# Running-sum rows read in six pieces, and two row copies of an attention and spectral-mix kernel cut into transfers of six, six and four partitions

## The chip, the core and the metric

The kernel runs on one core of one Trainium2 chip. The metric is the device time of one execution in microseconds (us), taken as the median of several runs. The core has the engines PE (TensorE), ACT (ScalarE), DVE (VectorE), POOL (GpSimd) and SP (SyncE), and 16 DMA engines that carry every transfer. A transfer is issued by SP or by POOL; the profile keeps the two apart as DMA queues: q1 "hardware_dynamic" holds what SP issues, q0 "software_dynamic" what POOL issues, and q8 and q14 "instruction" hold the chip's own fetching of instructions.

## What is computed

Inputs are `q`, `k`, `v` of shape (8 batches, 8 heads, 576 tokens, 64), `s` of shape (8, 8, 576), and the weights `w_r`, `w_i` (64 modes, 512, 512) and `w_ch` (512, 512), all float32. The reference, cut to what matters:

```python
cum = np.cumsum(np.maximum(s, 0), axis=-1)
bias = -(cum[:, :, :, None] - cum[:, :, None, :])
scores = where(causal, -1e9, q @ k.T / 8 + np.minimum(bias, 0))
x = softmax(scores) @ v                      # heads side by side: (8, 576, 512)
X = np.fft.rfft(x, axis=1)[:, :64]           # 64 modes of the tokens
Y = X * (w_r + 1j * w_i)                     # a complex 512x512 product per mode
u = x + np.fft.irfft(Y, n=576, axis=1)
out = u + np.maximum(u @ w_ch, 0)            # float32 (8, 576, 512)
```

The two mode weights are 134 MB of float32 and are read once.

## The kernel before, in words

**Attention, 32 steps (L591 to L625).** Step `n` works on one batch and two heads. `qt` and `kt` (two buffers each) hold the transposed q and k in partitions 0 to 63. Partition 64 of `qt` holds the negative running sum of `s` as an extra row, and partition 64 of `kt` holds ones, so that one product gives score and bias together (L397). ACT takes the exponential (L405), PE multiplies by v (L433), DVE divides (L438 to L448), and `fft` (L450) multiplies by sines and cosines and leaves the modes in `xs`.

**The running-sum row.** The sums are made once in `ncum_sb` (64 pairs of batch and head, 576 numbers of bf16). For steps 0 and 1 SP copies the rows from there (L345). L586 writes all of `ncum_sb` to `ncum_dram` in DRAM, and for each of the steps 2 to 31 `cum_rows` (L336) lets SP copy the step's two rows of 1152 bytes from DRAM into partition 64 of `qt` (L342). That copy waits until PE has read the old row out of the buffer; it is issued one step ahead.

**The weights.** The weights come in half chunks of 8 modes by 128 input channels (512 KB each as bf16), cast on the way. POOL issues them at L243 in the order of use into rings of 5 and 3 buffers, a load waiting until PE has read the buffer's old content. A list worked out ahead (L247 to L269) sets how many may be issued before each attention step. Each such load lies on all 16 DMA engines, 16 packets of 2048 bytes on each and a 4-byte packet that reports the end. `modes(g, c)` (L470) multiplies chunk `c` (8 chunks) of channel group `g` (4 groups).

**The end (L626 to L965).** Of the last channel group, chunks 0 to 5 are done in the loop at L862, chunk 6 at L883 and chunk 7 at L897. A chunk's product `yb` (128 rows: 16 mode rows by 8 batches, 512 columns) is transposed (L698), multiplied by `w_ch` (`y_times_wch`, L706) and stored as `vb`. For the inverse transform the rows have to lie as 16 partitions by 8 batches in `yv[partition, batch, which, column]`, where `which` is 0 for y and 1 for y times `w_ch`. `spread(c, which, rows)` (L511) makes that change of layout with one SP transfer, 128 pieces of 1024 bytes from 128 partitions to 16. It is called for `which` = 1 of chunks 4, 5, 6, 7 (L714, L915) and for `which` = 0 of chunks 6 and 7 (L506). Chunks 0 to 3, and `which` = 0 of chunks 4 and 5, go by PE instead (`gather`, L717).

**Order around the change.** SP issues in program order: the row copies, five small constants, then the spreads, then the stores of the result (L854, L857). PE's order in the end is written out: in the products of chunk 7 (`modes` with `meanwhile`), after the first half of the four groups of products (those with `w_r`), it runs `first_z` for the first two pairs of output tiles, which reads `yv` rows 0 to 95 with `which` = 1 (L773), that is chunks 0 to 5, then the third group of products, then `first_u`, then the fourth. All products of chunk 7 read weights that are loaded last: the two `w_r` halves, then `w_i` in four pieces of 256 KB.

Of the kernel before, what the change touches and what calls it, by code (L numbers as in the profile page):

```python
# [11 lines left out]
BF16 = mybir.dt.bfloat16  # L12
# [6 lines left out]
def kernel(  # L19
# [11 lines left out]
    nc = tc.nc  # L31
    B, H, S, D = q.shape
# [6 lines left out]
    NPAIR = B * H  # L39
# [6 lines left out]
    MC = 8  # L46
    NCK = NM // MC
# [12 lines left out]
    HP = P // 2  # L60
# [53 lines left out]
    auxpool = aux.enter_context(tc.tile_pool(name="aux_psum", bufs=2, space=PSUM, side="right"))  # L114

    dpool = ctx.enter_context(tc.tile_pool(name="dram", bufs=1, space=bass.MemoryType.DRAM))
    ncum_dram = dpool.tile([NPAIR, S + HP], BF16, name="ncum_dram")
    at = ExitStack()
    ap_ = at.enter_context(tc.tile_pool(name="attn", bufs=1))
    qkpool = at.enter_context(tc.tile_pool(name="qk_sb", bufs=2))  # L120
# [2 lines left out]
    ncum_sb = ap_.tile([NPAIR, S], BF16, name="ncum_sb")  # L123
    NQ = 2
    qt = [ap_.tile([P, 2, S], BF16, name=f"qt{i}") for i in range(NQ)]
# [25 lines left out]
    def loads_qk(n):  # L151

        if n >= N:
            return []
        g, b = divmod(n, B)
        hs = slice(2 * g, 2 * g + 2)
        t = loaded[n] = loaded[n + 1] = qkpool.tile([P, 2, R * D], BF16, name="qk2", tag="qk2")
        return [
            (
                t[HP * i : HP * i + HP, x0:x1],  # L160
                src[b + x0 : b + x1, hs].rearrange("b h (p r) d -> (h p) b (r d)", r=R),
            )
            for x0, x1 in ([(0, 2)] if n else [(0, 1), (1, 2)])
            for i, src in enumerate((q, k))
        ]

    def loads_v(n):

        if n >= N:
            return []  # L170
        g, b = divmod(n, B)
        return [
            (
                v2[n % NV][:, : 2 * NWN * W].rearrange("p (w h c) -> p w h c", w=NWN, h=2)[:, :, h, P:],
                v[b, 2 * g + h, : NF * P, :].rearrange("(w p r) d -> p w (r d)", p=P, r=2),
            )
            for h in range(2)
        ]

    def loads_tails(g):  # L180

        if g >= NG:
            return []
        return [
            (
                v4[g % 2][NL * h : NL * h + NL, :, :D],
                v[:, 2 * g + h, NF * P :, :].rearrange("b t d -> t b d"),
            )
            for h in range(2)
        ]  # L190
# [22 lines left out]
    def loads_w(upto):  # L213
        todo = []
        while 2 * len(wt) < min(upto, 2 * len(wq)):
            k = len(wt)
            g, c, ri = key = wq[k]
            i = ring_of(k)
            if i is None:
                halves_, t = early[k], whole[k] if k < len(whole) else None  # L220
            else:
                t = (wpool, wpool2)[i].tile([P, UM, DM], BF16, name="w_sb", tag="w")
                halves_ = [t[:, x * WM : x * WM + WM] for x in range(2)]
            if k == len(wq) - 1:
                t = None
            src = (moe_w_r, moe_w_i)[ri]
            for m0, m1, d in [(0, MC, t)] if t is not None else [(0, WM, halves_[0]), (WM, MC, halves_[1])]:
                for h in range(2):
                    first = 1 if ri == 1 and c == 0 and m0 + h == 0 else 0
                    todo.append((  # L230
                        d[HP * h : HP * h + HP, 2 * first :].rearrange("p (m q) e -> p m (q e)", q=2),
                        src[
                            c * MC + m0 + h + 2 * first : c * MC + m1 : 2, g * P : (g + 1) * P, :
                        ].rearrange("m (p q) e -> p m (q e)", q=2),
                    ))
            wt[key] = halves_
        return todo

    def load(*lists):

        todo = [((i + 0.5) / len(l), x) for l in lists for i, x in enumerate(l)]
        for _, (dst, src) in sorted(todo, key=lambda t: t[0]):
            nc.gpsimd.dma_start(out=dst, in_=src)  # L243
# [41 lines left out]
    with tc.tile_pool(name="cum_psum", bufs=1, space=PSUM) as cpsum:  # L285
# [3 lines left out]
        for t in qt + kt:  # L289
# [3 lines left out]
            out=cum, data0=spos, data1=zer, initial=0.0, op0=ALU.add, op1=ALU.add  # L293
# [16 lines left out]
        for x in range(2):  # L310
            rows = slice(NL * x, NL * x + NL)
            nc.vector.tensor_copy(
                out=cumt4[rows, :], in_=cumt_sb[rows, NK, x::2]
# [14 lines left out]
    def pad_p():  # L328
        for i in range(NP_):
            for x in range(NK):  # L330
                nc.vector.memset(
                    p_sb[i][:, poff[x] + S - x // 2 * W : poff[x + 1]], 1.0 if x in (0, NK - 1) else 0.0
                )


    def cum_rows(n):  # L336
        if n >= N:
            return
        g, b = divmod(n, B)
        p0 = b * H + 2 * g  # L340
        if n >= 2:
            nc.sync.dma_start(out=qt[n % NQ][D : D + 1, :, :], in_=ncum_dram[p0 : p0 + 2, :S].unsqueeze(0))  # L342
            return
        for h in range(2):
            nc.sync.dma_start(out=qt[n % NQ][D : D + 1, h, :], in_=ncum_sb[p0 + h : p0 + h + 1, :])  # L345

    def transposes(n, half):
        if n >= N:
            return
        src = loaded[n][:, n % 2, :].rearrange("p (r d) -> p r d", d=D)[:, half * RH : half * RH + RH]  # L350
        ps = trpool.tile([P, RH, 2 * RP], BF16, name="tr_ps", tag="tr")
        for r in range(RH):
            for i in range(2):
                rows = slice(HP * i, HP * i + HP)
                nc.tensor.transpose(ps[rows, r, :], src[rows, r, :], ident16[rows, rows])  # L355
        for i, dst in enumerate((qt, kt)):
            copy = (nc.vector.tensor_copy, nc.scalar.copy)[half * i]
            to = dst[n % NQ][:D].rearrange("d h (p r) -> d h p r", r=R)
            copy(  # L359
                out=to[:, :, :, half * RH : half * RH + RH],  # L360
                in_=ps[HP * i : HP * i + HP].rearrange("d r (h p) -> d h p r", h=2),
            )
# [147 lines left out]

    def spread(c, which, rows):  # L511

        nc.sync.dma_start(out=yv[16 * c : 16 * c + 16, :, which, :], in_=rows)

# [60 lines left out]
    def mode_products(n, half=None):  # L577
        cs = mode_steps.get(n, [])
        for c in cs if half is None else cs[2 * half : 2 * half + 2]:
            modes(c // NCK, c % NCK)  # L580

    with tc.tile_pool(name="sc_psum", bufs=2, space=PSUM) as scpool, \
            tc.tile_pool(name="tr_psum", bufs=1, space=PSUM) as trpool, \
            tc.tile_pool(name="av_psum", bufs=1, space=PSUM) as avpool:
        cum_rows(0)
        nc.sync.dma_start(out=ncum_dram[:, :S], in_=ncum_sb)  # L586
        transposes(0, 0)
        transposes(0, 1)
        load(loads_qk(2) + loads_v(2))
        pad_p()  # L590
        for n in range(N):  # L591
            if n in (0, 2):
                nc.vector.memset(xs_flat[n // 2].bitcast(FP32), 0.0)
            tails_due = loads_tails(n // B + 1)[n % B - 3 : n % B - 2] if 2 < n % B < 5 else []
            load((loads_qk(n + LA) if n % 2 else []) + loads_v(n + LA) + tails_due, loads_w(on_chip[n]))
            if n == N // 2 + 1:
                nc.gpsimd.dma_start(out=wch_sb, in_=moe_w_ch.rearrange("(dt p) e -> p dt e", p=P))
            cum_rows(n + 1)
            scores(n, 0)
            av(n - 1, 1)  # L600
            if n and n % B == 0:
                scores(n, 1)
                fft(n - 1)
                av(n, 0)
                mode_products(n, 0)
                transposes(n + 1, 0)
                mode_products(n, 1)
                transposes(n + 1, 1)
                continue
            mode_products(n)  # L610
            transposes(n + 1, 0)
            scores(n, 1)
            i = first_pairs[n - N + len(first_pairs)] if n >= N - len(first_pairs) else None
            if i is not None:
                first_transposed(i, 0)
            transposes(n + 1, 1)
            fft(n - 1)
            av(n, 0)
            if i is not None:
                first_product(i, 0)  # L620
                first_transposed(i, 1)
            if i is not None:
                first_product(i, 1)
        av(N - 1, 1)
        fft(N - 1)  # L625
# [5 lines left out]
    yv = finpool.tile([P, B, 2, DM], FP16, name="yv")  # L631
# [250 lines left out]
    c = NCK - 2  # L882
# [25 lines left out]
    for cols in halves:  # L908
        vp = auxpool.tile([P, DM // 2], FP32, name="v_ps", tag="aux")
        for dt in range(DT):  # L910
            nc.tensor.matmul(
                vp, yt[:, dt, :], wch_sb[:, dt, cols], start=(dt == 0), stop=(dt == DT - 1)
            )
        nc.vector.tensor_copy(out=vb[:, cols], in_=vp)
    spread(NCK - 1, 1, vb)  # L915
    for cols in halves:
        for i in range(NPRE):
# [78 lines left out]
```

## Time and profile before

| What | Value |
|---|---|
| median of 3 runs (lowest to highest) | 441.62 us (440.95 to 442.10) |
| the profiled execution: its own time / its span | 442.11 us / 440.3 us |
| PE, DVE, ACT, POOL busy | 77%, 57%, 51%, 39% of the span |
| DMA: bytes written, mean rate | 93.30 MB, 212 GB/s |
| HBM read, written | 163.58 MB, 9.51 MB |
| packets of POOL's queue q0 / of SP's queue q1 | 61424 / 7592 |
| packets of instruction queues q8 / q14 | 34 / 13 |
| granted TensorE clock, mean | 0.925 |

The span runs from the first to the last instruction; the 1.81 us beyond it lie around the execution. The page's second part cuts the span into 40 slices of 11 us, its fourth part follows the work that ended last back from the end, and its sixth lists DMA issues with their time to landing. Times in the text are us from the start of the span. Beside these views the trace keeps a record of each DMA packet (start, duration, size, queue, but not the DMA engine it ran on), of each landing (the increment of a transfer's semaphore that a DMA engine makes when its share is in place) and of the granted clock.

### The profile page before, as it was taken

What the parts mean: (1) busy time and instruction counts of PE and PEld (TensorE: products, weight loads), DVE (VectorE), ACT (ScalarE), POOL (GpSimd) and SP (SyncE); (2) the same over time, 40 slices, a digit from 0 to 9 for tenths busy, and PEclk for the clock granted to TensorE, in tenths of its full rate; (3) what the DMA queues carried; (4) which work ended last, traced back from release to release, by engine and by line L of the source; (5) the groups of instructions that cost most, each with busy time, mean ns of one, the idle gap of its engine ahead of it and who ended that gap; (6) DMA issues with size and microseconds to landing.
All of it is one profiled execution on the core that took longest, in us unless ns stands there. A gap on an engine that the chain in (4) does not pass through costs nothing.

```text
span 440.3 us, 10592 instructions
## 1 busy us (share of the span) xinstructions
PE 340.8 (77%) x4409; PEld 203.7 (46%) x4409; DVE 252.5 (57%) x574; ACT 226.0 (51%) x421; POOL 171.7 (39%) x257
## 2 busy tenths in 40 slices
PE   1588999899695977973939458899987797778995
PEld 1365666465463644641616125556554345432341
DVE  7667776677573555752715315766655344450795
ACT  1387878267463634860727024766651334330794
POOL 6555454424353444323444343433322212310293
PEclk9999999999988888995968767999999989996999
DMA  9999999999999999999999999999999999996498
GB/s 179 207 206 206 204 206 208 207 209 207 207 205 207 210 207 210 207 209 208 205 209 208 209 208 209 207 210 206 210 211 212 212 211 211 203 218 121 155 381 347
DMA packets 69063, 93.30 MB, mean 212 GB/s; under 512 B 25932, under 2 KB 27592, under 8 KB 69016
## 3 DMA queue, kind: packets, MB, share of 16 engines
q0 software_dynamic: 61424, 81.28, 104.6%
q1 hardware_dynamic: 7592, 11.36, 7.2%
q8 instruction: 34, 0.56, 0.5%
q14 instruction: 13, 0.11, 0.1%
HBM read 163.58 MB, written 9.51 MB: 393 GB/s over the span
## 4 chain that ended last, share of the span: by engine, by line
DMA 53%; PE 25%; DVE 15%; issue 3%; POOL 2%; ACT 1%; DVEq 0%; POOLq 0%
DMA w_sb<-in_moe_w_i_dram 21%; DMA w_sb<-in_moe_w_r_dram 17%; DMA qk<-in_k_dram 8%; DMA qk<-in_q_dram 5%; PE sc_ps L397 3%; DVE xs L468 3%; DVE qt L359 3%; PE z_ps L681 3%; PE yp L478 3%; DVE x_all L443 2%; PE av_ps L433 2%; PE sc_ps L391 2%; PE tr_ps L355 2%; DVE xt L553 2%; PE z_ps L773 2%
## 5 line engine op out<-in xcount | busy, mean ns | idle before, releaser
L405 ACT ACTIVATE p_sb<-sc_ps,cumt_sb 128x576 f16<-128x576 f32 (+1 forms) x256 | 141.9, 636 | 21.8 <-PE sc_ps L397 21.4
L397 PE MATMUL sc_ps<-qt,kt 128*128 128x512 bf16 (+2 forms) x384 | 76.8, 312 | 6.9 <-ACT kt L359 6.1
L243 POOL DMA_DIRECT2D v<-in_v_dram x72 | 51.4, 714 | 60.6 <-DMA w_sb<-in_moe_w_i_dram 12.8
L243 POOL DMA_DIRECT2D w_sb<-in_moe_w_i_dram x62 | 38.5, 623 | 89.2 <-DMA w_sb<-in_moe_w_i_dram 28.3
L359 DVE COPY qt<-tr_ps 64x576 bf16<-64x576 bf16 x64 | 47.8, 747 | 41.5 <-PE tr_ps L355 41.5
L478 PE MATMUL yp<-w_sb,xs 128*32 128x512 bf16 (+1 forms) x480 | 42.2, 431 | 29.1 <-DMA w_sb<-in_moe_w_i_dram 25.4
L355 PE MATMUL tr_ps<-ident,qk 64*64 64x64 bf16 x1152 | 34.3, 205 | 33.8 <-DMA qk<-in_k_dram 16.0
L243 POOL DMA_DIRECT2D w_sb<-in_moe_w_r_dram x60 | 37.4, 624 | 53.0 <-DMA w_sb<-in_moe_w_r_dram 33.3
L397 PEld LDWEIGHTS <-kt 128*128 128x128 bf16 x384 | 38.3, 105 | 34.5 <-ACT kt L359 12.8
L391 PE MATMUL sc_ps<-negm,ident 128*128 128x256 bf16 x256 | 53.5, 293 | 0.1
L355 PEld LDWEIGHTS <-qk 64*64 64x64 bf16 x1152 | 26.4, 117 | 51.7 <-DVE kt L359 20.3
L376 ACT ACTIVATE p<-sc_ps,cumt 128x64 f16<-128x64 f32 x32 | 10.1, 314 | 73.8 <-PE sc_ps L372 73.6
L433 PE MATMUL av_ps<-v,p_sb 128*128 128x65 f16 x1024 | 44.2, 197 | 1.8 <-DVE x_all L443 0.6
L359 ACT COPY kt<-tr_ps 64x576 bf16<-64x576 bf16 x32 | 22.8, 714 | 40.8 <-DVE qt L359 40.1
L433 PEld LDWEIGHTS <-p_sb 128*128 128x128 f16 x1024 | 37.4, 100 | 9.6 <-DVE x_all L443 5.4
L468 DVE CAST xs<-ft_ps 64x128 bf16<-64x128 f32 x128 | 36.7, 287 | 7.3 <-PE ft_ps L458 5.7
L478 PEld LDWEIGHTS <-xs 128*32 128x32 bf16 (+1 forms) x512 | 17.8, 146 | 46.0 <-DMA w_sb<-in_moe_w_i_dram 24.6
L438 DVE TENSOR_REDUCE den<-av_ps 128x5 f32<-128x10 f32 x64 | 10.8, 169 | 48.3 <-PE av_ps L433 47.3
L443 DVE TENSOR_TENSOR x_all<-av_ps,rcp 128x320 f16<-128x320 f32 x64 | 31.5, 492 | 2.2
L498 DVE TENSOR_TENSOR y_acc<-yp,y_acc 128x512 f32<-128x512 f32 x16 | 11.1, 692 | 29.2 <-PE yp L478 28.5
L539 ACT COPY z<-z_ps 128x512 f32<-128x512 f32 x22 | 12.9, 586 | 26.9 <-PE z_ps L571 14.2
L458 PE MATMUL ft_ps<-Ff_sb,x_all 128*64 128x192 f16 (+1 forms) x320 | 24.4, 266 | 1.0 <-DVE x_all L443 1.0
(107 smaller groups left out, 439.4 us busy)
## 6 DMA issues: line engine op xcount, KB each, us to landing
w_sb<-in_moe_w_r_dram POOLq DMA_DIRECT2D x60, 512.0 KB, 13.6
w_sb<-in_moe_w_i_dram POOLq DMA_DIRECT2D x55, 512.0 KB, 13.2
out_dram<-r_w SPq DMA_DIRECT2D x16, 512.0 KB
v<-in_v_dram POOLq DMA_DIRECT2D x72, 64.0 KB, 11.1
qk<-in_q_dram POOLq DMA_DIRECT2D x15, 288.0 KB, 12.0
qk<-in_k_dram POOLq DMA_DIRECT2D x15, 288.0 KB, 13.2
x_all<-in_moe_w_r_dram POOLq DMA_DIRECT2D x4, 512.0 KB, 8.4
w_sb<-in_moe_w_i_dram POOLq DMA_DIRECT2D x3, 384.0 KB, 12.7
```

The costliest lines, as they stand in the source:

```text
L243: nc.gpsimd.dma_start(out=dst, in_=src)
L355: nc.tensor.transpose(ps[rows, r, :], src[rows, r, :], ident16[rows, rows])
L359: copy(out=to[:, :, :, half * RH : half * RH + RH], in_=ps[HP * i : HP * i + HP].rearrange("d r (h p) -> d h p r", h=2),)
L391: nc.tensor.matmul(ps[:, bass.ds(w * S, W)], ident16, negm[:, bass.ts(r, W)], start=True, stop=False, skip_group_check=True,)
L397: nc.tensor.matmul(ps[:, c0 : c0 + i1 - i0], keys[:, w, r, :], qh[:, i0:i1], start=False, stop=True, skip_group_check=True,)
L405: nc.scalar.activation(out=pt[:, poff[x] : poff[x] + S - w * W], in_=ps[:, w * S : (w + 1) * S - w * W], func=ACTF.Exp, bias=cumt_sb[:, x, ...
L433: nc.tensor.matmul(ps[:, I, r : r + NCH], lhsT, rhs, start=(i == 0), stop=(i == len(todo) - 1), skip_group_check=True,)
L443: nc.vector.tensor_tensor(out=x_all[:, g, b, :, D * h : D * h + D], in0=ps[:, :, 1 : NCH], in1=rcp.unsqueeze(2).to_broadcast([P, NT, D]), ...
L458: nc.tensor.matmul(ps[HP * q_ : HP * q_ + HP].rearrange("p h f -> p (h f)"), x_all[:nT, g, b, T, q_::2], Ff_sb[:nT, T, :], start=(T == 0), ...
L468: nc.vector.tensor_copy(out=xs[g % 2][HP * h : HP * h + HP, q_, :, h, :, b, :], in_=a)
L478: nc.tensor.matmul(ps[32 * cg : 32 * cg + 32, :], cols[k0:, q_, 1 - ri, :, c * MC // 2 + cg], wt[(g, c, ri)][cg // 2][k0:, 2 * (cg % 2) + ...
L681: nc.tensor.matmul(zs[i, x], xts[i][:, x, dt, :], wch_sb[:, dt, :], start=(dt == 0), stop=(last and dt == DT - 1), skip_group_check=True,)
```

## The change

The copy `ncum_dram` in DRAM is laid out anew: each pair's 576 sums stand in three pieces of 192, 224 numbers apart. Writing it takes 192 pieces of 384 bytes instead of 64 of 1152. The copy into `qt` takes a step's two rows as six pieces of 384 bytes, where it took two of 1152. `spread` is cut for chunks below 6, which are chunks 4 and 5 of `which` = 1: three transfers with 6, 6 and 4 of the 16 target partitions (48, 48 and 32 source rows), where there was one with 16. SP issues 57 instructions instead of 54. Nothing is changed in what the other engines execute; the instructions that wait for a spread wait for three semaphores instead of one.

```diff
-    ncum_dram = dpool.tile([NPAIR, S + HP], BF16, name="ncum_dram")
+    NE6 = 6
+    CP = 2 * S // NE6
+    ncum_dram = dpool.tile([NPAIR, S // CP, CP + 32], BF16, name="ncum_dram")
...
-            nc.sync.dma_start(out=qt[n % NQ][D : D + 1, :, :], in_=ncum_dram[p0 : p0 + 2, :S].unsqueeze(0))
+            nc.sync.dma_start(
+                out=qt[n % NQ][D : D + 1, :, :],
+                in_=ncum_dram[p0 : p0 + 2, :, :CP].rearrange("h x t -> (h x) t"),
+            )
...
     def spread(c, which, rows):
 
-        nc.sync.dma_start(out=yv[16 * c : 16 * c + 16, :, which, :], in_=rows)
+        cuts = (0, 2 * MC) if c >= NCK - 2 else (0, NE6, 2 * NE6, 2 * MC)
+        for r0, r1 in zip(cuts, cuts[1:]):
+            nc.sync.dma_start(
+                out=yv[2 * MC * c + r0 : 2 * MC * c + r1, :, which, :], in_=rows[B * r0 : B * r1, :]
+            )
...
-        nc.sync.dma_start(out=ncum_dram[:, :S], in_=ncum_sb)
+        nc.sync.dma_start(
+            out=ncum_dram[:, :, :CP], in_=ncum_sb.rearrange("c (x t) -> c x t", t=CP)
+        )
```

## The prediction, made before the result was known

> **What bounds the kernel now.** I read the page's slices first. The DMA row is full from the first microseconds to about 402 us, while no compute engine is (PE is highest, 77%):
>
> ```profile
> PEclk9999999999988888995968767999999989996999
> DMA  9999999999999999999999999999999999996498
> ...
> q0 software_dynamic: 61424, 81.28, 104.6%
> q1 hardware_dynamic: 7592, 11.36, 7.2%
> q8 instruction: 34, 0.56, 0.5%
> ```
>
> So the weight stream of POOL sets the pace, with SP's queue and the instruction fetches beside it on the same DMA engines. Next I asked who waits for the last weights, in the chain of waits from 379 us on:
>
> ```profile
> 382.36 0.77 POOL w_sb L243 x2
> 383.13 0.44 issue
> 383.57 15.64 DMA w_sb<-in_moe_w_r_dram
> 399.21 0.14 issue
> 399.35 1.09 PE yp L478 x6
> 400.44 0.96 PE z_ps L773 x2
> ...
> 404.11 1.00 PE yp L478 x4
> ...
> 406.55 0.60 PE yp L478 x4
> ```
>
> The columns are start, length, what. The second `w_r` half of chunk 7 lands at 399.21; from 399.35 PE works without a gap to 407.15, and the rest of the kernel hangs on that. The weights used after it (last landing 405.13, needed at 406.55) have 1.4 us to spare. PE had been idle for 1.87 us before 399.35 (its last product, v_ps L709, ends at 397.48), so an earlier landing is worth its full amount up to 1.87 us.
>
> Then the landings. A weight load lands 16 times, once per DMA engine. For loads issued at 34.36, 367.91 and 383.57, sorted (us; the bars are mine):
>
> ```
> 34.36 41.43 41.52 41.59 41.61 41.62 41.80 | 41.89 41.92 | 41.93 41.97 41.98 42.15 42.27 42.82 42.84 43.17
> 367.91 382.86 382.91 382.94 383.44 383.76 384.09 | 385.31 385.42 | 386.58 386.78 387.09 387.22 387.39 387.41 387.46 387.48
> 383.57 394.84 395.00 395.00 395.06 395.12 395.49 | 396.25 396.68 | 397.35 397.73 398.00 398.18 398.21 398.22 398.24 399.21
> ```
>
> A load is placed only when its **slowest** engine is done. Over the kernel the engines have drifted into six early ones, a pair, and eight late ones. The packet records say why. A row copy of L342 lands on two engines; its 1152-byte packet holds the next weight packet off by 60 ns, its report packet by 22: 30 copies x 82 ns = 2.5 us on one fixed pair. From the first row to the second the pair fell behind the six by 1.7 us (from 0.31 to 2.03, means), with 27 copies between: 2.2 by that price. The 34 instruction fetches (16 KB, nearly 1 us each) repeat their durations with a period of eight (974, 961, 893, 892, 949, 945, 935, 974 ns), so they seem to go round eight engines: the late ones.
>
> **The change part by part.**
>
> *The spreads of chunks 4 and 5.* These two run inside the wait for the last weights:
>
> ```profile
> 384.21 6.46 SPq L513 DMA_DIRECT2D yv<-v_sb  x2
> ...
> q0 software_dynamic: 248, 0.48, 93.1%
> q1 hardware_dynamic: 144, 0.13, 18.1%
> ```
>
> (the first line is from the timeline, the others from the DMA queues at 388 to 390.7 us: SP's 128 pieces and 16 reports pass among the weight packets). Now each lands 16 times, so each DMA engine carries 8 pieces. Weight packets start 154 ns apart on one engine; with pieces between they start 208 apart: 54 ns a piece. Per engine and spread 8 x 54 + 22 for the report = 0.45 us, for both 0.91. A check: the eight late engines land on average at 387.18 and 398.14 in the lower rows, 10.96 us for four loads, where undisturbed loads land 2.48 apart (9.92): 1.04 too long, the 0.91 and something of a fetch at 390.25.
>
> A copy of two rows lands on 2 engines and a transfer to 16 partitions on 16, so I take it that 6, 6 and 4 partitions land on 6, 6 and 4, always from the same end of the engines, where the row pair is too. Then ten engines carry no piece (**-0.91 us**), two carry 16 per spread instead of 8 (16 pieces and 2 reports more in all, +0.9 us), and four carry 24 (32 pieces and 4 reports more, 32 x 54 + 4 x 22 = +1.8 us). If those six are the pair and four of the early six, the late eight gain 0.91 and the others have room, worked out next.
>
> *The rows in six pieces.* The pair is relieved of 60 + 22 ns per copy and six engines get a 384-byte piece. Packets of that size took 22 to 35 ns at the start of the kernel: with the report 44 to 57 ns, x 30 = 1.3 to 1.7 us on six engines. The pair gains about 1.0, the four lose 1.5. Room: at 367.91's row the early six stand 3.4 to 4.6 us ahead of the last. They ran dry at 382.9 to 384.1, as the next load was issued at 381.76 and first landed at 386.71 (2.5 of work, so begun at 384.2), which swallows about 1 of the 1.5. In the last row they come to about 395.0 + 0.5 + 1.8 = 397.3, the pair to 396.5 - 1.0 + 1.8 = 397.3, the late ones to 399.21 - 0.91 = 398.3. Still last: the late ones. So this edit buys nothing by itself; it makes room for the other. The rows themselves land 4.5 us after issue, one step (6.6 us or more) ahead, and in the waits of PE no L397 waits for them: their cover is some 5 us. Writing `ncum_dram` is 12 x 22 instead of 4 x 64 ns per engine: nothing, 15 us before the first read (7.7 and 22.9).
>
> *SP.* Four issues more at 0.55 to 0.6 us. SP's next work after 391.9 is the y spread of chunk 6 at 395.34: 3 us of cover. Without it that spread would be late, which PE reads only after 411.
>
> *The new wait.* `first_z` waits for three transfers of chunk 5 instead of one; behind it on PE stands all that follows. Now chunk 5's pieces start at 393.94 (3.27 us after the issue ends) and land by 396.42. After: 24 pieces in one line at 208 ns end at 398.93, reports and landing (0.5) make 399.4 to 399.5. PE will want them at 398.45 + 1.09 = 399.54. That fits by 0.1 us. From below: faster pieces when weights run dry, no loss; from above, see the second rival. I take 0 to 0.1 lost.
>
> **Sum:** 442.11 (execution; span 440.3 and 1.81 around it) - 0.91 + 0.05 = 441.25. The profiled run lies 0.49 above the median, so for the median 441.62 - 0.86, rounded **440.7**.
>
> **A rule against it.** The Trainium skill, "DMA: Bandwidth & Descriptors", Rules for kernel authors, says to put a multiple of 16 outermost, since a smaller outermost dimension confines the DMA to that many engines. By it alone the cut triples a spread's time on its engines (1.67 to 5.0 us by this trace's 208 ns) for nothing. The same page (why a DMA increments its semaphore by 16) says that such a transfer takes the lowest-numbered engines; the trace agrees as far as the same pair is always hit, but it gives no numbers.
>
> **Rivals.**
>
> *Slower: the pieces hit late engines.* Nothing here shows that the other four of the six belong to the early group; only that pair and fetch engines are distinct, and that neighbours would be natural. If one of the four is late, it comes at 398.24 + 1.5 + 1.8 = 401.5 instead of 399.21: PE starts 2.3 us later, up to 3.3 if it is the straggler. Time 443.9 to 444.9. It decides as soon as one such engine has less than 3.3 us of lead. Chance 0.12.
>
> *The pieces come too late for `first_z`.* If two weight packets pass per piece (54 + 308 = 362 ns), 24 pieces end at 402.6: PE then waits past 400.44 for some 2.7 us, 444.2. Against it: 1:1 was seen on all engines. Chance 0.05; each 0.1 us beyond 399.54 costs 0.1.
>
> *More than forecast: the clock.* In these stages (span, PE, PEld, DVE, ACT, POOL busy, then granted clock):
>
> ```profile
> 387.50:399.20 11.70, 7.28 (x86) 3.34 (x84) 6.04 (x9) 2.89 (x5) 0.60 (x1) 0.96 1.12 218
> 399.20:407.20 8.00, 7.78 (x34) 2.12 (x34) 0.03 (x1) 0.00 (x0) 0.00 (x0) 0.63 0.44 92
> ```
>
> PE, having idled, got half the clock from 398.33 to 405.15. If the shorter pause (0.97 for 1.87 us) avoids that, PE's part shrinks until the last weights bind (405.13 - 0.9 = 404.2 against 405.65): up to 1.4 us more, 439.3. Chance 0.16. This state may also differ from run to run (440.95 to 442.10).
>
> *Nothing.* The straggler, 1 us behind the other late engines, carries a fetch; if fetches move with the change, the 0.91 may drown: 441.6. Chance 0.07.
>
> **How the numbers follow.** Forecast 0.60, range 440.0 to 441.4. This kernel's measurement can tell about 0.3% (1.3 us) from no change, so the likeliest gain of 0.9 us lies inside it. Faster by more, so below 440.3: 0.20 of the forecast's 0.60 and 0.15 of the clock case, together 0.35. Slower: 0.12 + 0.05 = 0.17. Within: the remaining 0.40 of the forecast, 0.07 and 0.01, together 0.48. The range takes in clock case and half of the late-piece case: 439.3 to 443.0.
>
> **What would show it.** Right: the load now landing last at 399.21 lands at about 398.3; its 16 landings are closer together, with no pair apart; PE's idle time before yp L478 drops to 1.0 us; SP's pieces land on 6, 6 and 4 engines. Wrong: PE waits at z_ps L773 for yv; the first landings of a load lie as before while the last move out; or the slices of the tail change.

## The result, and the profile after

| | before | after |
|---|---|---|
| median (lowest to highest, executions) | 441.88 us (440.32 to 442.75, 13) | 443.82 us (442.57 to 445.22, 13) |
| ratio to before | | 1.0046, 95% interval 1.0034 to 1.0058 |
| first profiled execution: time / span | 442.11 / 440.3 us | 442.57 / 440.8 us |

The change costs 0.46%, 1.9 us; the interval leaves out 1, so this is a loss, if a small one. The first trace of the changed kernel is of its quickest execution, so what it shows is less than the whole.

From the page of the changed kernel, the clock, the DMA row and the queues:

```profile
PEclk9999999999987988895977758999997999996998
DMA  9999999999999999999999999999999999995498
...
q0 software_dynamic: 61424, 81.28, 104.4%
q1 hardware_dynamic: 7960, 11.36, 7.3%
q8 instruction: 34, 0.56, 0.5%
```

SP's queue has 368 packets more (7592 before), the shares have moved by 0.2 points at most, and the DMA row is as full as before. SP issues 76 transfers in the trace instead of 72, four more and not three. Averages over the span cannot show what happened; the chain of waits does (start, length, what):

```profile
382.29 17.80 DMA w_sb<-in_moe_w_r_dram
400.10 0.14 issue
400.23 1.09 PE yp L483 x7
401.32 0.97 PE z_ps L784 x2
...
406.76 0.60 PE yp L483 x4
```

The same load still ends the wait, but it lands at 400.10, not 399.21, and the forecast was 398.3. The timeline of PE has PE's idle time before it (in brackets), first before the change and then after it; the forecast was 1.0:

```profile
399.35 1.09 PE L478 MATMUL yp<-w_sb,xs 128*32 128x512 bf16 x8 [1.87 <-DMA w_sb<-in_moe_w_r_dram]
400.23 1.09 PE L483 MATMUL yp<-w_sb,xs 128*32 128x512 bf16 x8 [2.88 <-DMA w_sb<-in_moe_w_r_dram]
```

The stages of the prediction, cut at the new landing (span, PE, PEld, DVE, ACT, POOL busy, clock, DMA share, GB/s):

```profile
387.50:400.10 12.60, 6.42 (x68) 2.73 (x68) 5.83 (x9) 2.89 (x5) 0.59 (x1) 0.90 1.11 213
400.10:407.40 7.30, 7.10 (x34) 2.11 (x34) 0.02 (x1) 0.00 (x0) 0.00 (x0) 0.70 0.35 73
```

The first stage is 0.9 us longer, at nearly the same rate (213 and 218 GB/s). The second is 0.7 shorter with the same 34 matmuls, at a clock of 0.70 instead of 0.63: in this execution most of the delay is paid back by the clock, which is taken up below.

Now the landings of that load, one per DMA engine, sorted (us; the bars are mine). The first row was shown in the prediction:

```
before   394.84 395.00 395.00 395.06 395.12 395.49 | 396.25 396.68 | 397.35 397.73 398.00 398.18 398.21 398.22 398.24 | 399.21
after    393.18 393.23 393.69 395.12 395.44 396.57 | 397.57 397.73 397.87 397.90 397.95 398.12 398.12 398.79 | 399.88 400.10
```

The late pack ends about where it ended before (the prediction wanted it 0.91 earlier), and **two engines now stand two microseconds behind it**; one of them decides. Before, one engine alone stood that far back, 1.7 us.

### The profile page after: what moved, and what is told of

Same layout as the page of the kernel before. It is cut to its first block, busy times and chain, and to the rows that moved or that the text cites. A ratio compares the mean times of both kernels' runs of the same rounds, so it can differ in the third digit from the quotient of the medians.

```text
span 440.8 us, 10555 instructions
## 1 busy us (share of the span) xinstructions
PE 338.7 (77%) x4362; PEld 203.9 (46%) x4409; DVE 252.7 (57%) x574; ACT 226.3 (51%) x421; POOL 171.3 (39%) x257
## 4 chain that ended last, share of the span: by engine, by line
DMA 50%; PE 25%; DVE 16%; issue 4%; ACT 2%; POOL 2%; DVEq 0%; POOLq 0%
DMA w_sb<-in_moe_w_i_dram 25%; DMA w_sb<-in_moe_w_r_dram 16%; DMA qk<-in_k_dram 5%; PE yp L483 4%; DVE xs L473 3%; DVE qt L364 3%; PE sc_ps L402 3%; DMA qk<-in_q_dram 3%; DVE x_all L448 2%; PE z_ps L692 2%; PE av_ps L438 2%; PE sc_ps L396 2%; PE tr_ps L360 2%; DVE xt L562 2%; PE z_ps L784 2%
## 5 line engine op out<-in xcount | busy, mean ns | idle before, releaser
L402 PE MATMUL sc_ps<-qt,kt 128*128 128x320 bf16 (+2 forms) x337 | 66.4, 302 | 10.3 <-ACT kt L364 5.8
```

The lines of the kernel that those rows point to most:

```text
L402: nc.tensor.matmul(ps[:, c0 : c0 + i1 - i0], keys[:, w, r, :], qh[:, i0:i1], start=False, stop=True, skip_group_check=True,)
```

## The experiments

The prediction's rival "the pieces hit late engines" had nearly come true in size (443.9 to 444.9 for it, 443.82 measured). Three theories went into the runs. **A**: among the six engines that carry the small pieces are some of the late ones, so the load lands later. **B**: the pieces of chunk 5 land too late and PE waits for them at `z_ps`, or the small transfers cost as such. **C**: the clock; PE idles longer and works longer at half speed. A began as "one late engine, the last of all" and became "three" after the first four runs; the expectations below carry the version of their time. The packet records support one, as is shown below.

Each run is compared with runs of the kernel before on the same chip; "load" is the second `w_r` half of chunk 7.

**The rows alone.** The change with `spread` as before.

```diff
-        cuts = (0, 2 * MC) if c >= NCK - 2 else (0, NE6, 2 * NE6, 2 * MC)
+        cuts = (0, 2 * MC)
```

> Only the rows in six pieces; the spreads are whole as before. Theory A (one of the six engines that carry small pieces is a late one, the last of all): that engine gets 30 x 35 to 57 ns = 1.0 to 1.7 us more row work and draws the stream of loads back; the load issued near 368 lands last about 0.4 to 0.6 us later than before's 387.48, as it did in the changed kernel (388.05), the second w_r half of chunk 7 at 399.6 to 399.9 (before 399.21), time +0.3 to +0.7 us. Theory B (the small transfers of the spreads cost as such, whatever engines they land on): nothing, within 0.2 us of before. Theory C (the clock): landings as before, and a time that differs only by how long the granted clock stays at half.

Measured: 441.50 us against 441.40, ratio 1.0002 (0.9990 to 1.0014). In time the rows cost nothing and bring nothing, as the prediction had it; A's +0.3 to +0.7 for them failed, B's zero held. The trace is a lesson by itself: its load landed at 400.09, as late as in the changed kernel and even later than A said (399.6 to 399.9), yet the time was 441.30. PE, at half clock, was busy with v_ps until 400.47, and the clock came back at 402.08. One trace does not tell whether the rows by themselves make the load late in most executions.

**The spreads alone.** Before, with chunks 4 and 5 cut 6, 6, 4.

```diff
-        nc.sync.dma_start(out=yv[16 * c : 16 * c + 16, :, which, :], in_=rows)
+        cuts = (0, 2 * MC) if c >= NCK - 2 else (0, 6, 12, 2 * MC)
+        for r0, r1 in zip(cuts, cuts[1:]):
+            nc.sync.dma_start(
+                out=yv[2 * MC * c + r0 : 2 * MC * c + r1, :, which, :], in_=rows[B * r0 : B * r1, :]
+            )
```

> Only the spreads of chunks 4 and 5 in 6, 6 and 4; rows as before in two pieces on the pair. Theory A: the late engine among the six carries 16 pieces per spread instead of 8, 16 x 54 + 2 x 22 ns = +0.9 us, the late ones outside the six lose 0.9; the last landing of the second w_r half lies at 399.1 (carrier in the middle of the late group) to 400.1 (carrier is the last), time -0.1 to +0.9 us; together with rows_only it adds up to the changed kernel's +1.9 within 0.7. Theory B: the whole +1.9 us is here, with chunk 5's pieces landing at 399.6 to 400.2 and PE waiting for them at z_ps, or the load landing at 400.1 as in the changed kernel. If all six had room, as the prediction took it: load at 398.3, time -0.8.

Measured: 443.71 against 441.40, ratio 1.0051 (1.0035 to 1.0066). A loss as large as the whole is here. In the trace the load lands at 400.30 and chunk 5's last piece at 400.39. It is not two engines that stand apart here: five land between 399.67 and 400.30.

**Four engines instead of six.** Rows in four pieces, both spreads in four transfers of 4 partitions (one execution).

```diff
-    NE6 = 6
+    NE6 = 4
...
-        cuts = (0, 2 * MC) if c >= NCK - 2 else (0, NE6, 2 * NE6, 2 * MC)
+        cuts = (0, 2 * MC) if c >= NCK - 2 else (0, 4, 8, 12, 2 * MC)
```

> Four engines in place of six everywhere: rows in four pieces of 576 bytes, both spreads in four transfers of 4 partitions, so 64 pieces of the spreads on each of four engines. Theory A with a late engine as fifth or sixth: the late engines carry no piece, the second w_r half lands at 398.2 to 398.6 (before 399.21, changed kernel 400.10); but chunk 5's pieces, 32 in a line, land near 401.7 to 402.5 (24 took 6.4 to 7.0 us from 393.2 on), so PE waits for yv at z_ps, time +1.3 to +2.2 us. If a late engine is already among the first four: the load at 400.1 or later. Theory B: no earlier landing of the load than in the changed kernel.

Measured: 445.98. From its chain of waits:

```profile
398.52 4.76 DMA yv<-v_sb
403.28 0.34 issue
403.62 1.01 PE z_ps L784 x2
```

Now PE waits for `yv`, as expected. More telling are the 16 landings of the load:

```
four     394.60 394.66 394.75 395.42 | 397.12 397.17 397.28 397.30 397.34 397.40 397.48 397.65 | 398.04 398.28 398.72 399.51
```

Eight engines land within 0.5 us around 397.34, their mean. That is 9.30 us after the load four places ahead was complete (388.04); in the three traces of before the late pack, without its straggler, comes 10.51, 9.95 and 10.46 us after it. The pack has gained 1.0 us on average. Counted from the mean of the late eight of that earlier load instead, it is 10.08 against 10.80, 10.55 and 10.80, a gain of 0.6. Either way it goes towards the 0.91 that the prediction gives to engines without pieces: **these eight carry none**, so no late engine is among the first four. Of the engines that come first, four land as if untouched (394.60 to 395.42).

**Which engines they are.** Before, with seven extra copies to an unused place in DRAM, of 1 to 7 partitions of 1280 bytes.

```diff
+    probe = dpool.tile([N, 8, NT * P + 64], FP16, name="probe")
...
+            if n > N - B:
+                kp = n - (N - B)
+                nc.sync.dma_start(
+                    out=probe[n, :kp, : NT * P], in_=x_all[:kp, NG - 1, (n - 1) % B, :, :].rearrange("p t d -> p (t d)")
+                )
```

> The kernel before with seven extra copies to an unused place in DRAM, at attention steps 25 to 31, of 1, 2, ... 7 partitions of 1280 bytes. They land on 1 to 7 engines, so the k-th engine of the order is held up by 8-k copies of about 60 + 22 ns. Theory A: the landings of the load issued near 368 and the reports of the loads behind it show the first three or four tagged engines in the early group and the pair, the fifth or sixth tag in the late group. The prediction's assumption: six tags on the pair and early engines, and only the seventh late. The time is that of before within 0.5 us.

Measured: 441.28 in one execution, inside the 440.04 to 442.73 of before: no cost that shows. An engine that works without a break sends its report packets 2.486 us apart, load after load, so the 16 can be followed one by one. The copy of six partitions passes at 318.0 to 318.3 us, and exactly six engines fall behind, by 0.05 to 0.07 us. Two report intervals each, engines in the order in which the load issued at 305.67 landed on them (us; "fetch" marks an engine that an instruction fetch at 321.64 holds up as well):

```
place  1    2    3    4    5    6    7    8    9    10   11   12     13   14   15   16
       4.97 5.04 5.04 4.97 4.97 5.03 5.04 5.04 4.97 4.97 4.97 fetch  5.04 4.97 4.97 4.97
```

Places 2, 3, 6, 7, 8 and 13. Five of the six belong to the eight that land first, among them both engines of the row pair: the row copy at 310.43 holds up places 6 and 8. **One, place 13, belongs to the late half.** An expectation below has places 1, 6, 7, 8, 9 and 13 (counted there from 0) and three late ones; that took 1 for 2, whose reports lie 25 ns apart, and 9 for 3, 6 ns apart. But place 3 lands 5.05 us apart from the load issued at 305.67 to the one at 308.61 (314.86 and 319.91), place 9 4.97 (317.36 and 322.33). The landings of the change and of `four` say the same as the packets: with `four`, four early engines come as if untouched, in all five traces of the change three (in the first 393.18 to 393.69, the next at 395.12). So of the fifth and sixth engine one is early and one is late.

**Chunk 4 alone, twice.** The cut only for `c == NCK - 4`, rows as before.

> Only the spread of chunk 4 in 6, 6 and 4; chunk 5 whole, rows as before. Theory A (three of the six engines that a six-partition transfer lands on belong to the late half, as the extra copies showed: places 0, 5, 6, 7, 8 and 12 of 16 by landing): the late ones among the six carry 16 or 24 pieces of chunk 4 instead of 8, +0.45 to +0.9 us, the other late ones lose 0.45; the second w_r half lands 0.4 to 0.9 later, time +0.4 to +1.0 us, that is a part of the +2.2 of both. Theory B (the pieces of chunk 5 come too late for PE): nothing, since chunk 5 is whole; time within 0.3 us of before or up to 0.4 below.

> Chunk 4 alone in 6, 6 and 4, a second comparison: if the gain is real, -0.2 to -0.9 us (ratio 0.998 to 0.9995); if it was chance, within 0.2 us of before.

Measured: 441.31 against 441.81, ratio 0.9986 (0.9975 to 0.9997), and then 441.64 against 441.55, ratio 1.0001 (0.9989 to 1.0014). The gain did not come back on the second chip: an interval that just misses 1 is no find. The load landed at 399.06 and 398.98. A's +0.4 to +1.0 failed: by the prediction's price chunk 4's pieces bring 8 more to the late engine, 0.45 us, which need not reach past the engine that stands behind the others anyway (1.6 to 1.8 us in the three traces of before).

**Chunk 4 in four transfers of 4.**

> Chunk 4's spread in four transfers of 4 partitions, chunk 5 whole, rows as before: 32 pieces on each of four engines, none on twelve. Theory A: of the four engines one or two belong to the late half; they get 24 x 54 + 3 x 22 ns = +1.4 us instead of +0.9 at most, so the second w_r half lands at 399.3 to 400.0 and the time is 0 to +0.8 us of before, above c4_only. If only the twelve relieved engines count (they lose 0.45 us): -0.4 to -0.8 us as in c4_only.

Measured: 441.46 against 441.55, ratio 1.0000 (0.9987 to 1.0014). It tells nothing apart.

**Chunk 5 alone.** The cut only for `c == NCK - 3`.

> Only the spread of chunk 5 in 6, 6 and 4; chunk 4 whole, rows as before. Theory A: as for chunk 4, +0.4 to +1.0 us, and the two together make the +2.2. Theory B: nearly all of the +2.2 is here; the third transfer lands at 399.5 to 400.5 and PE waits for it at z_ps, or the pieces of the three transfers run into the last weights and stretch their packets.

Measured: 442.41 against 441.81, ratio 1.0024 (1.0008 to 1.0040). In its trace (443.89 us) the load lands at 400.77, and the chain shows the second rival of the prediction at work:

```profile
392.44 9.75 DMA yv<-v_sb
402.18 0.05 issue
402.23 1.03 PE z_ps L777 x2
```

PE had come there at 402.00 (400.77 + 0.14 + 1.09), so that wait cost 0.2 us, not the whole. For the late load A has no price: 8 pieces more are 0.45 us here as with chunk 4 alone, where the load landed 1.7 us earlier.

**The price of late pieces by themselves.** Before, with chunk 5's whole spread issued behind chunk 6's y spread.

```diff
+    spread(NCK - 3, 1, vb5)
```

(ahead of the second chunk's transposes, at L883, and left out of `y_times_wch` for chunk 5)

> The kernel before, with the whole spread of chunk 5 issued after chunk 6's y spread, some 6 us later: it lands on all 16 engines at about 401 to 402.5. No piece of it lies ahead of the second w_r half, which lands at 398.5 to 398.9. Theory B: PE waits at z_ps for yv until 401 to 402.5, and the time is +0.7 to +2 us: the price of late pieces alone. Theory A: no loss, 0 to -0.5 us.

Measured: 445.52 against 441.78, ratio 1.0086 (1.0065 to 1.0107). In PE's timeline, the load's wait is short and the one for `yv` long (idle time in brackets):

```profile
398.81 1.09 PE L478 MATMUL yp<-w_sb,xs 128*32 128x512 bf16 x8 [0.69 <-DMA w_sb<-in_moe_w_r_dram]
402.96 1.01 PE L774 MATMUL z_ps<-yv,G_sb 96*128 96x512 f16 x2 [3.07 <-DMA yv<-v_sb]
```

With no piece of chunk 5 ahead of it, the load lands at 398.67, 0.5 us before its mean of 399.22 in before: what B costs when it is really there, and what 8 pieces per engine are worth.

**Taking B away.** PE's order changed in both kernels: `first_u` before the third group of products, `first_z` behind it, so that chunk 5 is read some 4 us later.

```diff
-    yb = modes(NG - 1, NCK - 1, {2: lambda: (first_z(0), first_z(1)), 3: first_u})
+    yb = modes(NG - 1, NCK - 1, {2: first_u, 3: lambda: (first_z(0), first_z(1))})
```

> The kernel before, with PE's first_z moved behind the third group of products of chunk 7 and first_u in its place: the rows of chunk 5 are then read about 2 us later (at about 402.5 to 403). Baseline for the next run. Since the third group may wait for its w_i quarters (landed 401.5 and 402.3), time between 0 and +1.5 us of before.

> The changed kernel with the same reordering of PE. The pieces land as in the changed kernel (chunk 5's third transfer at 400 to 402.2), but PE wants them only at about 402.5. Theory B (PE waits for chunk 5's pieces in most executions, though not in the two that were traced): the distance to the reordered kernel before shrinks from +1.9 to 0 to +0.6 us. Theory A (the loads land later, since late engines carry the pieces): the distance stays at +1 to +2, as the w_i loads are late by the same.

Measured against the same runs of before: 441.30, ratio 0.9995 (0.9977 to 1.0012), and 443.22, ratio 1.0040 (1.0025 to 1.0054). The distance stays at 1.9 us though `first_z` no longer waits; from the chain of the reordered changed kernel:

```profile
382.27 18.43 DMA w_sb<-in_moe_w_r_dram
400.69 0.14 issue
400.83 1.08 PE yp L483 x6
...
405.19 0.54 PE z_ps L784 x2
```

Chunk 5's last piece had landed at 400.52, 4.7 us before PE reads it. **The wait of B is not the cause.** The load lands at 400.69, against 399.50 in the reordered kernel before. B's other half, that the small transfers cost as such, is not ruled out by this; it comes back with the long packets at the end.

**Rows and chunk 4.** The change with chunk 5 whole.

> The change without its cut of chunk 5: rows in six pieces, chunk 4 in 6, 6 and 4, chunk 5 whole. c4_only took 0.14% (0.6 us) off and the rows nothing; so 440.9 to 441.6, that is -0.2 to -0.8 us against before, and 2 to 2.5 below the change. If the loss of the change lay in the sum of all pieces on six engines, +0.5 or more.

Measured: 442.58 against 441.78, ratio 1.0022 (1.0009 to 1.0036). Slower by 0.8 us where the parts gave nothing; in its trace (441.76, one of its quickest) the load lands at 399.38, as in before. I have no cause for it.

**More traces of the two kernels.**

> The kernel before, once more, for a second trace: how far do the landing of the second w_r half (399.21) and the half clock of TensorE (398.33 to 405.15) move from one execution to the next? If the clock alone sets the spread of 440.0 to 442.7, the landings agree within 0.3 us and the time follows the length of half clock between 399 and 407.

> The kernel before, third trace: the second w_r half at 399.0 to 399.5, chunk 5's pieces by 396.5, time 440.5 to 442.5.

> The changed kernel, once more, for a second trace, since its first was of its quickest execution (442.57 against a median of 443.82). Theory A: the second w_r half lands at 400 to 401.5, and PE stands still before it by the difference. Theory C: the landing agrees with the first trace (400.10) and the difference in time is that of the half clock behind it.

> The changed kernel, third trace. In an execution near the median (443.8), theory A: the second w_r half lands at 400.7 to 401.8, and PE goes on with it 0.14 us later; theory B: it lands near 400.1, and PE stands at z_ps until a landing of yv at 401.5 to 402.5; theory C: landings near 400.1 and 400.2, and the clock at half for 2 us or more longer between 400 and 408.

> The changed kernel, fourth trace, with the same three outcomes as the third.

> The changed kernel, fifth trace, with the same three outcomes as the third.

With the first of each, in us:

| trace | time | load lands | last two engines behind the pack | half clock | y of chunk 7 done |
|---|---|---|---|---|---|
| before | 442.11 | 399.21 | 0.8, 1.7 | 398.33 to 405.15 | 407.13 |
| before, second | 441.47 | 399.08 | 0.7, 1.6 | 396.93 to 403.75 | 406.48 |
| before, third | 442.57 | 399.36 | 0.7, 1.8 | 395.69 to 405.93 | 407.58 |
| after | 442.57 | 400.10 | 2.0, 2.2 | 397.59 to 404.42 | 407.33 |
| after, second | 442.18 | 400.04 | 1.9, 2.1 | 400.92 to 404.33 | 406.96 |
| after, third | 443.46 | 400.46 | 1.3, 2.6 | 398.74 to 405.56 | 408.23 |
| after, fourth | 444.15 | 401.06 | 2.0, 3.1 | 396.25 to 406.49 | 408.77 |
| after, fifth | 443.61 | 400.21 | 1.8, 2.0 | 396.40 to 406.64 | 408.37 |

The pack is the seven engines ahead of the one before the last two, their mean. In before one engine stands 1.6 us or more behind it, in four of the five traces of the change two do, in the third one. Whether they are the same engines from trace to trace the landings do not tell, nor which of them carries pieces; in the reordered kernel before, without any cut, two stand apart as well (1.5 and 2.1). B shows in one of the five, the third, by 0.28 us ("issue" is the wait for chunk 5's last piece, landed at 401.75):

```profile
400.60 1.08 PE yp L483 x6
401.68 0.28 issue
401.95 1.01 PE z_ps L784 x2
```

In the other four the pieces were there (399.98 to 400.27) before PE asked (400.84 to 402.30).

All eight times follow one rule: PE starts 0.14 after the load, needs 4.9 to 5.1 us at full clock to the end of chunk 7's products, and loses half of whatever part of that lies in the half clock; from there it is 35.0 us to the end in before and 35.2 to 35.4 in after. For before: 399.35 + 4.87 + 5.80/2 = 407.13; for the fifth of after: 400.35 + 4.88 + 6.29/2 = 408.37. So the mean difference of the traces, 443.19 - 442.05 = 1.14 us, comes apart as

- the load, 400.37 - 399.22: **+1.16**
- half clock, overlap 4.83 instead of 5.59 us: -0.38
- PE at full clock, with B's wait in it, 5.01 instead of 4.91: +0.10
- the end: +0.27.

The last is in every one of the 13 traces with cut spreads (35.2 to 36.0 us) and in one of the seven without (before reordered, 35.24; the others 34.98 to 35.06). In the first pair of traces it lies behind DVE's last work on the chain (435.65 + 0.60 in before, 435.86 + 0.60 in after): 4.1 and 4.3 us to the end of the span. Where it comes from no run shows.

C is not the cause: the half clock took less from the traced executions of after, not more, and the mean granted clock over all timed executions is 0.910 in after and 0.910 to 0.911 in before. It makes most of the spread from one execution to the next.

## Why the prediction was wrong, point by point

**What bounds the kernel** was right: the load's slowest engine, and PE behind it.

**The step that failed** is "If those six are the pair and four of the early six". It was a condition, and the sum went on as if it were known. Six partitions do land on six engines, and the pair is among them; but one of the six belongs to the late eight. By the prediction's own price that one carries 16 pieces per spread in place of 8: 16 x 54 + 2 x 22 ns = +0.91 us where the sum had -0.91. With its row pieces (1.5 in the rival's sum) it would come at about 398.24 + 1.5 + 0.9 = 400.6, an estimate. Measured, the load lands at 400.04 to 401.06, 400.37 on average: 1.16 us later and not 0.9 earlier.

**-0.91 for engines without pieces**, the second term that failed, went to the other late engines. With `four` 0.6 to 1.0 of it is seen. In the change it is not: the pack lies at 397.9 to 398.2, where the late engines of before, without the last, lie at 397.9 to 398.0. Counted as with `four`, from the late eight of the load four ahead, that is 10.60 us on average against 10.72.

**The rival's price** (2.3 to 3.3 us for a late engine with 24 pieces per spread and row pieces on top) was too high: the sixth engine, like the fifth, gets only two of the three transfers, and the rows by themselves cost the time nothing measurable.

**The pair** was read too simply: the two engines that land between the six and the late eight need not be the ones that the row copies hold up; in `probe` these are places 6 and 8.

**The rows buy nothing by themselves**: right (1.0002). **SP's issues**: 0.66 to 0.84 us each, not 0.55 to 0.6,

```profile
382.94 8.45 SPq L520 DMA_DIRECT2D yv<-v_sb  x6
395.21 0.62 SPq L520 DMA_DIRECT2D yv<-y_sb  x1
```

but covered: the y spread of chunk 6 leaves at 395.21, in before at 395.34. In the sum itself, 441.62 - 0.86 is 440.76, so 440.8 and not 440.7; nothing hangs on it.

**The new wait** was mis-sized: chunk 5's last piece lands at 399.98 to 401.75, not at 399.4 to 399.5. In the first trace the pieces start at 393.21 and the last lands at 400.19; less the prediction's 0.5 for report and landing, that is 0.27 us for each of 24, not 0.208. The wait would have eaten half of the forecast gain or more, had there been one; as the load is late too, it costs 0.28 us in one trace of five.

**The clock** case did not come: with the load later, no trace of the change shows a shorter pause.

**What stays open.** The traces explain 1.14 us of a median difference of 1.94 (1.5 to 2.6 by the interval). The five traced executions of after average 443.19, below its median, so the rest may be sampling; no run here shows it. The parts also do not add up: chunk 4 nothing, chunk 5 0.24%, both 0.51%. That the load is late, and that this is what PE pays for, is shown; how much of the 1.16 us comes from the pieces on the late engine is not. The long packets described at the end are a rival that no run takes away: they go with the late loads from kernel to kernel, and they could explain what the pieces do not, the missing gain of the pack and the 400.30 of `spread_only`, where the late engine has no row pieces (398.24 + 0.9 = 399.1 by the price) and the long packets are at their most, 17.2 us or 1.1 us per engine.

The Trainium skill, "DMA: Bandwidth & Descriptors", Rules for kernel authors, warned of a small outermost dimension, which confines a transfer to that many engines; the runs side with it (1.0051 for the spreads alone). The same page (Why a DMA increments its semaphore by 16 and not by 1) has such a transfer on the lowest-numbered engines. The runs tell engines by their landings and not by number; they fit it as far as the two engines of a row copy are among the six of the copy of six partitions in `probe`.

## What to carry to other kernels

When a stream over many engines waits for its slowest, a transfer that lands on few engines is only worth having if you know where those engines stand. Find out first, with a few extra copies of rising size whose delay shows in the spacing of the report packets; it costs a run and no time. And when a prediction says "if", give the other case the weight of what is not known: here nothing spoke for four early engines except that it would be convenient.

None of the versions tried beats the kernel before: chunk 4 alone, 0.14% faster in one comparison, is equal to it in the second.

## What the runs showed of the hardware that was not expected

- **The granted clock comes in pieces of 3.41 us.** Every half-clock stretch near the last load is 3.41, 6.83 or 10.24 us long, in before as in after, and begins anywhere between 393.5 and 401.1. Where PE did not wait for `yv`, it took 0.9 to 3.2 us out of an execution (overlap 1.85 to 6.42), more than the change itself. One trace with a late load can be quicker than one with an early load, as `rows_only` was; compare landings, not one pair of times.
- **Packets get longer when chunk 5 is cut in sixes.** A weight packet usually takes 173 ns. Between 394 and 400 us, the time by which weight packets and pieces exceed their usual length sums to 1.9 to 17.2 us over 16 engines in all eight traces with chunk 5 in sixes, and to 0.7 at most in the other twelve, `four` with its transfers of four partitions among them. Within the change it does not go with the landing of the load (fourth trace 4.5 us and the latest landing, fifth 11.8 us and 400.21), and I have no cause for it.
- **About 0.3 us more at the end** of every kernel with the additional transfers, and of one without them, as told above.
